# Moving a weight conversion from ScalarE to GpSimd and shifting it in the order of steps

## The chip, the cores and the metric

The kernel runs on one core of a Trainium2 chip. The metric is the device time of one execution in microseconds; shorter is better. The engines that matter are TensorE (PE), VectorE (DVE), ScalarE (ACT) and GpSimd (POOL); SyncE (SP) issues the transfers.

## The reference

Causal attention with 2 batches, 12 heads, 448 tokens and 64 columns a head, then two feed-forward layers on the 896 x 768 result:

```python
attn = softmax(where(causal, q @ k.T / 8, -1e9)); x = attn @ v
h = x @ w_in                 # 768 -> 2048
y = (h * cos(h)) @ w_out     # 2048 -> 768
out = ((y @ w_a) * (y @ w_b)) @ w_out2   # 768 -> 1536 -> 768
```

The weights arrive as 64-bit floats, everything else as 32-bit floats.

## The kernel before

A product is made of three matmul terms on reduced 32-bit floats (fp32r): each operand is split into a high part `hi` and a rest `lo`, and hi*hi, hi*lo and lo*hi are summed in PSUM (`product`, line 160).

The weights come in 70 chunks of up to 128 x 768 numbers, each as pairs of 32-bit words, and are converted on the chip. One chunk goes through these functions: `w_load` (DMA by SP's queue), `w_scale` (ACT rescales the high word in place), `w_shift` and `w_pack` (DVE brings the mantissa bits together in the low word), `w_sign` (DVE adds the sign), `w_hi` (ACT copies the low word, read as a float, into `w_hi`, rounded to fp32r), and `w_lo` (POOL subtracts `w_hi` from it, and then the load of chunk i + 3 is issued). So `w_sign`, `w_hi` and `w_lo` of a chunk are a chain. There are three `w_raw` buffers and four pairs `w_hi`, `w_lo`.

`w_pump` (line 135) makes the next half of this work: on one call shift and pack of a chunk, on the next one sign, hi and lo of this chunk and scale of the chunk behind it.

Attention runs first, in steps written out by hand (`CYCLE`, line 464): four steps, called banks, for each of 12 pairs of heads. Each engine takes its instructions in the order in which they are written. `scores` puts products into four PSUM banks, one for each of the steps; `row_max` (DVE) reads them, `exps` (ACT) makes the exponentials and sums, `recip` (DVE) the reciprocals, `scale_p` (POOL) multiplies, `transposes` (PE) turns the result into two PSUM banks, `keep` (DVE and ACT) copies these out, and `values` (PE) multiplies by v. The seven row tiles of a pair are in two groups, even tiles (6, 0, 4, 2: the first two banks) and odd ones (5, 3, 1: the last two). `scale_p`, `transposes` and `keep` exist for either group.

`ASIDE` (line 483) puts other work behind the `CYCLE` work of a step. Chunk 0 is converted at steps 5 to 10. `PUMPS` (line 495) names the steps of four calls of `w_pump`: shift and pack of chunk 1; sign, hi, lo of chunk 1 and scale of chunk 2; shift and pack of chunk 2; sign, hi, lo of chunk 2 and scale of chunk 3. `ROWS` puts parts of the first three w_in products between the steps from 44 on; the third of them, which reads chunk 2, begins at step 53. The last scores are issued at step 44.

Behind attention come the rest of w_in with the cosine gate, w_out, w_a with w_b, and w_out2, each with a call of `w_pump` per unit of work.

Of the kernel before, what the change touches and what calls it, by code (L numbers as in the profile page):

```python
# [12 lines left out]
ACTF = mybir.ActivationFunctionType  # L13
ALU = mybir.AluOpType
# [7 lines left out]
def f32(ap):  # L22
    return ap.bitcast(F32)
# [3 lines left out]
def tile_causal_attention_cos_gate_bilinear(  # L27
# [16 lines left out]
    nc = tc.nc  # L44
# [18 lines left out]
    def act_tiles(pool, tag, kind, b, n):  # L63
        return [
            tuple(pool.tile([P, S], F32R, tag=f"{tag}{b}_{t}{part}", name=f"{kind}{b}_{t}{part}") for part in ("hi", "lo"))
            for t in range(n)
        ]


    CHUNK = 6 * P  # L70
    queue = []
    for kind, w in (("in", w_in), ("out", w_out), ("ab", None), ("o2", w_o2)):
        if kind == "ab":
# [2 lines left out]
        for f in range(w.shape[0]):  # L76
            for j, o in enumerate(range(0, w.shape[2], CHUNK)):
                queue.append((kind, f, j, w[f][:, o : min(o + CHUNK, w.shape[2])]))
    raw, chunks = {}, {}
    pumps = itertools.count(3)  # L80

    def w_raw():
        return wp.tile([P, CHUNK, 2], I32, tag="w_raw", name="w_raw", bufs=3)

# [35 lines left out]
    def w_hi(i):  # L120
        if i < len(queue):
            kind, f, j, src = queue[i]
            n = src.shape[1]
            pair = tuple(wp.tile([P, CHUNK], F32R, tag=f"w_{p}", name=f"w_{p}", bufs=4) for p in ("hi", "lo"))
            nc.scalar.activation(pair[0][:, :n], f32(raw[i][:, :, 0]), ACTF.Copy)  # L125
            chunks[kind, f, j] = (*pair, n // P)

    def w_lo(i, engine):
# [6 lines left out]
    def w_pump():  # L135

        i, odd = divmod(next(pumps), 2)
        if odd:
            w_shift(i)
            w_pack(i)  # L140
        else:
            w_sign(i - 1)
            w_hi(i - 1)
            w_lo(i - 1, nc.gpsimd)
            w_scale(i)
# [38 lines left out]
        yield ps  # L184


    EARLY = 3
    PARTS = 6
    units = [(f, b) for b in range(B) for f in range(EARLY)]
    units += [(f, b) for f in range(EARLY, N_IN) for b in range(B)]  # L190
    stages, partial = {}, {}
# [26 lines left out]
    def square(u):  # L218
        if u in stages:
            r = stages[u][1]  # L220
            nc.scalar.activation(r, r, ACTF.Square, scale=2.0**0.5)  # L221

    def gate(u):
        if u in stages:
            ps, r = stages[u]
            nc.vector.scalar_tensor_tensor(out=r, in0=r, scalar=1.0, in1=ps, op0=ALU.subtract, op1=ALU.mult)  # L226
# [47 lines left out]
    with ExitStack() as actx:  # L274
# [6 lines left out]
        for o in (0, S):  # L281
            for e in range(2):
                half = mask[e * D : (e + 1) * D, o : o + D]
                nc.gpsimd.affine_select(
                    out=half,
# [172 lines left out]
        def at(fn, i):  # L458
# [27 lines left out]
            (8, w_pack, 0),  # L486
            (9, w_sign, 0),
            (10, w_hi, 0),
            (10, w_lo, 0, nc.gpsimd),
            (14, w_load, 1),  # L490
# [1 line left out]
            (22, w_scale, 1),  # L492
        ]
        ROWS = [44, 45, 46, 47, 48, 49, 50, 51, 51, 52, 52, 53, 53, 54, 55, 56, 57, 57]
        PUMPS = [24, 28, 32, 36]
        WARM = 4
        for k, step in enumerate(ROWS):
            ASIDE.append((step, rows_part, k // PARTS))
        for step in PUMPS:
            ASIDE.append((step, w_pump))  # L500
# [19 lines left out]
    with tc.manual_schedule():  # L520
        g = [act_tiles(g_pool, "g", "g", b, N_IN) for b in range(B)]
        for u in range(EARLY):
            gate(u - 2)
# [3 lines left out]
            square(u - 1)  # L527
            if u < EARLY - 1:
                w_pump()
        for u in range(EARLY, len(units) + 2):  # L530
            gate(u - 2)
# [81 lines left out]
```

## Time and profile before

| what | value |
|---|---|
| median of 3 runs | 590.97 us (589.45 to 591.11) |
| the profiled execution's own time | 589.5 us |
| its span in the trace | 587.7 us |
| PE busy | 575.7 us, 98% of the span |
| DVE busy | 360.3 us, 61% |
| ACT busy | 270.0 us, 46% |
| POOL busy | 217.9 us, 37% |
| granted TensorE clock | 1.000 |

An engine's busy time is the time in which one of its instructions is in flight; a matmul that waits for an operand inside a merged row can count as busy.

### The profile page before, as it was taken

How to read it: one execution, taken by the hardware profiler on the slowest of the kernel's cores; microseconds unless marked ns; L12 is line 12 of the kernel's file. 1: busy time of each engine (PE TensorE's matmuls, PEld its weight loads, DVE VectorE, ACT ScalarE, POOL GpSimd, SP SyncE). 2: the span in 40 equal slices, each digit the busy share in tenths (PEclk: the TensorE clock that was granted, in tenths of full speed). 3: DMA queues.
4: the chain of work that ended last, by engine and by line, in shares of the span. 5: the costliest groups of instructions: out<-in, count | busy, mean ns of one | idle time of the engine just before them, and what ended most of it. 6: DMA issues, size and time to landing. Idle time of an engine off the chain costs nothing.

```text
span 587.7 us, 8729 instructions
## 1 busy us (share of the span) xinstructions
PE 575.7 (98%) x3310; PEld 512.7 (87%) x3310; DVE 360.3 (61%) x599; ACT 270.0 (46%) x534; POOL 217.9 (37%) x197
## 2 busy tenths in 40 slices
PE   8898899999999999999999999999999999999997
PEld 6565578999999999999999999999999999999996
DVE  4877764777777776644564666666666666555500
ACT  5787865777777742322232333333333333322100
POOL 4656641666666653322232222222222222322200
PEclk9999999999999999999999999999999999999999
DMA  8662410333333244332432433333323333443000
GB/s 315 255 211 83 172 45 0 109 108 107 109 107 109 90 126 161 94 113 82 144 116 99 159 109 108 107 109 107 109 107 108 109 108 108 138 139 138 32 32 31
DMA packets 15449, 67.80 MB, mean 115 GB/s; under 512 B 1712, under 2 KB 3376, under 8 KB 15408
## 3 DMA queue, kind: packets, MB, share of 16 engines
q1 hardware_dynamic: 15408, 67.25, 33.8%
q8 instruction: 26, 0.43, 0.3%
q14 instruction: 15, 0.12, 0.1%
HBM read 64.49 MB, written 2.75 MB: 114 GB/s over the span
## 4 chain that ended last, share of the span: by engine, by line
PE 93%; DVE 2%; POOL 2%; ACT 1%; issue 1%; DVEq 0%; POOLq 0%
PE h L169 20%; PE y L169 20%; PE o L169 15%; PE a L169 15%; PE b L169 15%; PE xa L434 3%; PE pt L407 2%; PE s L334 2%; ACT p L378 1%; POOL w_lo L132 1%; POOL p L393 1%; DVE p L357 1%; PE warm L454 1%; DVE pp L420 0%; DVE w_raw L103 0%
## 5 line engine op out<-in xcount | busy, mean ns | idle before, releaser
L132 POOL TENSOR_TENSOR w_lo<-w_raw,w_hi 128x768 fp32r<-128x768 f32 (+1 forms) x70 | 128.9, 1842 | 279.8 <-ACT w_hi L125 209.6
L109 DVE SCALAR_TENSOR_TENSOR w_raw<-w_raw 128x768 int32<-128x768 int32 (+1 forms) x70 | 124.4, 1777 | 63.2 <-ACT w_raw L98 62.3
L125 ACT ACTIVATE w_hi<-w_raw 128x768 fp32r<-128x768 f32 (+1 forms) x70 | 62.7, 896 | 163.7 <-DVE w_raw L116 100.6
L116 DVE SCALAR_TENSOR_TENSOR w_raw<-w_raw 128x768 int32<-128x768 int32 (+1 forms) x70 | 65.9, 942 | 0.4
L98 ACT ACTIVATE w_raw<-w_raw 128x768 f32<-128x768 f32 (+1 forms) x70 | 61.5, 878 | 0.0
L393 POOL TENSOR_SCALAR p<-p,sums 128x448 f32<-128x448 f32 (+6 forms) x84 | 41.8, 517 | 24.3 <-DVE sums L386 16.1
L378 ACT ACTIVATE p<-p,mn 128x448 f32<-128x448 f32 (+6 forms) x84 | 41.8, 499 | 13.3 <-DVE mn L357 13.3
L103 DVE TENSOR_SCALAR w_raw<-w_raw 128x768 int32<-128x768 int32 (+1 forms) x70 | 42.8, 611 | 0.0
L357 DVE CUSTOM_DVE_ANT_0 p<-s,mask 128x448 f32<-128x448 f32 (+6 forms) x84 | 32.1, 417 | 15.0 <-PE pt L407 9.7
L210 DVE SCALAR_TENSOR_TENSOR r<-k,h 128x448 f32<-128x448 int32 x32 | 19.8, 618 | 26.0 <-ACT k L209 25.6
L334 PE MATMUL s<-qk_raw 64*64 64x64 f32 (+6 forms) x336 | 30.7, 411 | 2.4 <-DVE mn L357 2.3
L563 DVE COPY o<-o 128x448 f32<-128x448 f32 x12 | 7.5, 625 | 35.3 <-PE o L169 35.3
L334 PEld LDWEIGHTS s<-qk_raw 64*64 64x64 f32 x336 | 15.4, 139 | 15.6 <-DVE mn L357 6.6
L407 PE MATMUL pt<-ident,p 128*128 128x128 f32 x168 | 23.6, 280 | 4.8 <-POOL p L393 3.8
L209 ACT ACTIVATE k<-h 128x448 int32<-128x448 f32 x32 | 17.3, 540 | 18.6 <-PE h L169 17.8
L407 PEld LDWEIGHTS pt<-ident,p 128*128 128x128 f32 x168 | 18.1, 140 | 8.3 <-POOL p L393 5.1
L555 DVE TENSOR_TENSOR c<-a,bs 128x448 f32<-128x448 f32 x24 | 15.0, 625 | 15.4 <-PE a L169 15.4
L434 PEld LDWEIGHTS xa<-pp,v 128*64 128x64 f32 x336 | 16.1, 137 | 9.0 <-issue 6.9
L434 PE MATMUL xa<-pp,v 128*64 128x64 f32 (+3 forms) x336 | 23.8, 293 | 0.0
L226 DVE SCALAR_TENSOR_TENSOR r<-r,h 128x448 f32<-128x448 f32 x32 | 19.5, 611 | 1.5 <-ACT r L221 1.5
L216 ACT ACTIVATE r<-r 128x448 f32<-128x448 f32 x32 | 18.3, 573 | 0.0
L221 ACT ACTIVATE r<-r 128x448 f32<-128x448 f32 x32 | 18.3, 571 | 0.0
(376 smaller groups left out, 1560.9 us busy)
## 6 DMA issues: line engine op xcount, KB each, us to landing
w_raw<-in_w_in SPq DMA_DIRECT2D x16, 768.0 KB, 4.3
w_raw<-in_w_out SPq DMA_DIRECT2D x12, 768.0 KB, 4.2
w_raw<-in_w_b SPq DMA_DIRECT2D x12, 768.0 KB, 4.2
w_raw<-in_w_a SPq DMA_DIRECT2D x12, 768.0 KB, 4.4
w_raw<-in_w_o SPq DMA_DIRECT2D x12, 768.0 KB, 4.3
v<-in_v SPq DMA_DIRECT2D x12, 448.0 KB, 5.8
qk_raw<-in_qk SPq DMA_DIRECT2D x11, 448.0 KB, 5.9
w_raw<-in_w_out SPq DMA_DIRECT2D x6, 512.0 KB, 3.8
```

Of the source, the lines that this page charges most:

```text
L98: nc.scalar.activation(high, high, ACTF.Copy, scale=2.0**-112)
L103: nc.vector.tensor_single_scalar(low, low, 29, op=ALU.logical_shift_right)
L109: nc.vector.scalar_tensor_tensor(out=low, in0=high, scalar=3, in1=low, op0=ALU.logical_shift_left, op1=ALU.bitwise_or)
L116: nc.vector.scalar_tensor_tensor(out=low, in0=high, scalar=SIGN, in1=low, op0=ALU.bitwise_and, op1=ALU.bitwise_or)
L125: nc.scalar.activation(pair[0][:, :n], f32(raw[i][:, :, 0]), ACTF.Copy)
L132: engine.tensor_tensor(out=lo[:, :n], in0=f32(raw.pop(i)[:, :, 0]), in1=f32(hi)[:, :n], op=ALU.subtract)
L169: nc.tensor.matmul(ps, w[:, c * P : (c + 1) * P], acts[t + c][part], start=t == 0 and i == 0, stop=t + k == n and i == len(terms) - 1,)
L334: nc.tensor.matmul(T["s", i + c][q, o : o + WIDTH[j]], t[h, Q_COL[j] : Q_COL[j] + D], t[h, FIRST[j] : FIRST[j] + WIDTH[j]], start=True, st ...
L378: nc.scalar.activation(t, t, ACTF.Exp, bias=T["mn", n][:, c], scale=-1.0, accum_out=row_sum(n, j))
L393: nc.gpsimd.tensor_scalar(out=t, in0=t, scalar1=row_sum(n, j), scalar2=1.0, op0=ALU.mult, op1=ALU.mult)
L407: nc.tensor.transpose(dst, p_bufs[n % N_P][:, o : o + P], ident)
L434: nc.tensor.matmul(ps[e * D : (e + 1) * D, o * D : w * D], t[:, k, e], p[:, :, :, q].rearrange("p s l q -> p (s l) q") if k < 3 else p[:, ...
```

## The change

`w_hi` of the first three chunks runs on POOL as a `tensor_scalar` that multiplies by 1 twice; the other 67 stay on ACT. `PUMPS` becomes 26, 32, 46, 49. `EARLY` is the constant 3 that also counts the w_in products begun inside attention; its line moves up.

```diff
+    EARLY = 3
     queue = []
...
             pair = tuple(wp.tile([P, CHUNK], F32R, tag=f"w_{p}", name=f"w_{p}", bufs=4) for p in ("hi", "lo"))
-            nc.scalar.activation(pair[0][:, :n], f32(raw[i][:, :, 0]), ACTF.Copy)
+            src = f32(raw[i][:, :, 0])
+            if i < EARLY:
+                nc.gpsimd.tensor_scalar(out=pair[0][:, :n], in0=src, scalar1=1.0, scalar2=1.0, op0=ALU.mult, op1=ALU.mult)
+            else:
+                nc.scalar.activation(pair[0][:, :n], src, ACTF.Copy)
...
-    EARLY = 3
...
-        PUMPS = [24, 28, 32, 36]
+        PUMPS = [26, 32, 46, 49]
```

## Rows read from the trace of the kernel before

**Rows 1.** The page: chain that ended last; costliest groups (busy us, mean ns).

```profile
PE 93%; DVE 2%; POOL 2%; ACT 1%; issue 1%; DVEq 0%; POOLq 0%
...
L103 DVE TENSOR_SCALAR w_raw<-w_raw 128x768 int32<-128x768 int32 (+1 forms) x70 | 42.8, 611 | 0.0
```

**Rows 2.** Busy time of each engine by stretch, with its column line.

```profile
core 0: us, PE busy (x) PEld busy (x) DVE busy (x) ACT busy (x) POOL busy (x), PEclk, DMA share, GB/s
...
27.40:95.40 68.00, 64.65 (x693) 44.65 (x689) 45.71 (x181) 47.39 (x152) 34.06 (x64) 1.00 0.32 111
95.40:110.00 14.60, 14.60 (x74) 13.54 (x73) 11.10 (x16) 12.13 (x22) 5.87 (x4) 1.00 0.16 55
```

**Rows 3.** Timeline of PE: start, length, line, [idle before <- releaser].

```profile
33.11 1.98 PE L434 MATMUL xa<-pp,v 128*64 128x384 f32 x28
...
38.87 1.98 PE L434 MATMUL xa<-pp,v 128*64 128x384 f32 x28
...
46.50 1.98 PE L434 MATMUL xa<-pp,v 128*64 128x384 f32 x28
...
53.13 1.98 PE L434 MATMUL xa<-pp,v 128*64 128x384 f32 x28
55.68 0.98 PE L407 MATMUL pt<-ident,p 128*128 128x128 f32 x7 [0.57 <-POOL p L393]
...
61.41 1.98 PE L434 MATMUL xa<-pp,v 128*64 128x384 f32 x28
...
68.04 1.98 PE L434 MATMUL xa<-pp,v 128*64 128x384 f32 x28
...
74.45 1.98 PE L434 MATMUL xa<-pp,v 128*64 128x384 f32 x28
```

**Rows 4.** Timeline of DVE, step 24 (chunk 1, shift and pack).

```profile
42.79 0.81 DVE L103 TENSOR_SCALAR w_raw<-w_raw 128x768 int32<-128x768 int32 x1
43.64 1.11 DVE L109 SCALAR_TENSOR_TENSOR w_raw<-w_raw 128x768 int32<-128x768 int32 x1
```

**Rows 5.** Timeline, step 28: chunk 1, sign on DVE and lo on POOL.

```profile
50.42 0.95 DVE L116 SCALAR_TENSOR_TENSOR w_raw<-w_raw 128x768 int32<-128x768 int32 x1
...
52.40 1.86 POOL L132 TENSOR_TENSOR w_lo<-w_raw,w_hi 128x768 fp32r<-128x768 f32 x1 [3.63 <-ACT w_hi L125]
```

**Rows 6.** POOL's groups by form (busy us, mean ns of one).

```profile
L132 POOL TENSOR_TENSOR w_lo<-w_raw,w_hi 128x768 fp32r<-128x768 f32 x64 | 120.7, 1885 | 266.5 <-ACT w_hi L125 196.3 <-PE y L169 42.6 <-PE o L169 25.1
...
L393 POOL TENSOR_SCALAR p<-p,sums 128x448 f32<-128x448 f32 x12 | 7.7, 642 | 16.0 <-DVE sums L386 8.8 <-ACT p L378 7.2
...
L393 POOL TENSOR_SCALAR p<-p,sums 128x64 f32<-128x64 f32 x12 | 4.2, 346 | 0.0
```

**Rows 7.** Timeline of DVE, POOL and PE, steps 9 to 13 (chunk 0).

```profile
18.61 0.95 DVE L116 SCALAR_TENSOR_TENSOR w_raw<-w_raw 128x768 int32<-128x768 int32 x1
...
21.68 1.86 POOL L132 TENSOR_TENSOR w_lo<-w_raw,w_hi 128x768 fp32r<-128x768 f32 x1 [2.99 <-ACT w_hi L125]
...
23.70 0.53 DVE L420 COPY pp<-pt 128x384 f32<-128x384 f32 x1
...
25.41 0.98 PE L407 MATMUL pt<-ident,p 128*128 128x128 f32 x7 [1.96 <-POOL p L393]
```

**Rows 8.** Timeline of an undisturbed pair: ACT, DVE and PE.

```profile
34.33 0.51 ACT L378 ACTIVATE p<-p,mn 128x256 f32<-128x256 f32 x1 [0.42 <-DVE mn L357]
...
35.71 0.60 ACT L418 ACTIVATE pp<-pt 128x512 f32<-128x512 f32 x1 [0.39 <-PE pt L407]
...
36.15 0.23 DVE L357 CUSTOM_DVE_ANT_0 p<-s,mask 128x64 f32<-128x64 f32 x1 [1.10 <-PE pt L407]
...
36.74 1.04 PE L407 MATMUL pt<-ident,p 128*128 128x128 f32 x7
```

**Rows 9.** Timeline of ACT and PE, steps 48, 49 and 53.

```profile
83.53 0.60 ACT L418 ACTIVATE pp<-pt 128x512 f32<-128x512 f32 x1 [1.10 <-PE pt L407]
...
84.87 0.93 PE L407 MATMUL pt<-ident,p 128*128 128x128 f32 x7
...
92.75 0.36 PE L169 MATMUL h<-x_0hi,w_hi 128*128 128x448 f32 x1
```

## The prediction

> **What bounds the kernel now.** I read the page first: the chain of waits is 93% TensorE, with 2% DVE, 2% POOL and 1% ACT [rows 1]. TensorE is therefore the bound, and a change off it is worth only the TensorE idle time that it removes. The table of windows then says where that idle time is: from 95.4 us on, in the stretch shown and in those after it up to the last outputs, TensorE is busy the whole time; between 27.4 and 95.4 us it is busy 64.65 of 68.0 us [rows 2]. So whatever attention ends earlier, the program ends earlier, as long as the projections behind it stay fed.
>
> Third came the timeline of TensorE, read by the start of `values` (line 434), one per pair of heads [rows 3]. An undisturbed pair takes 38.87 - 33.11 = 5.76 us. The five pairs after it take 7.63, 6.63, 8.28, 6.63 and 6.41 us: 35.58 us, against 28.80, so 6.78 us are lost. (The idle remarks alone show less, since a matmul that waits inside a merged row counts as busy.) These five pairs are where chunks 1 and 2 are converted, at PUMPS steps 24, 28, 32, 36. Last I read DVE, ACT and POOL around those steps, to see which instruction each lost microsecond follows.
>
> Per chunk there are three losses. Shift and pack (first pump) hold DVE between `keep` and the `row_max` of tiles 4 and 2, whose PSUM bank the next scores need: 42.79 to 44.67, 1.87 us lost out of 7.63 [rows 3, 4]. Sign (second pump) takes DVE at the same place: 0.87 us lost (6.63). Then ACT's hi, and POOL's lo behind it, keep POOL from the odd `scale_p`, and the next transposes start late: 0.65 us (6.41 - 5.76; for chunk 1 this is the 55.68 row). The 8.28 is 0.65 of chunk 1 and 1.87 of chunk 2, to the hundredth. Sum: 3.39 us per chunk.
>
> **The change, part by part.**
>
> *Chunk 2's shift and pack, from step 32 to 46.* It removes 1.87 us. At step 46 no scores are left to be issued, and w_in matmuls stand between TensorE's attention pieces. What is late next: the `row_max` and Exp of tiles 3 and 1, and behind them ACT's copy of transposes (`keep`), whose bank the next transposes need. That copy sat waiting 1.10 us for TensorE at 83.53; a delay of 1.85 makes it 0.75 late, 84.28, and it ends at 84.88; the transposes start at 84.87 [rows 9]. So cost 0, with no margin; if the Exp is later than I read, it costs up to 1.87 again.
>
> *Chunk 2's sign, hi, lo, from step 36 to 49.* Removes 0.87 + 0.65. At step 49 DVE does sign behind `x_hi` and `x_lo`, about half a microsecond each after that copy, so from 85.9 to 86.85 (0.95, as at 50.42); POOL has only the last `scale_p` left ahead of it, and hi and lo end near 86.85 + 0.9 + 1.9 = 89.65 on the old clock. The first matmul that reads this chunk stands at 92.75 [rows 9], lo only later: slack above 3 us. Cost 0. Chunk 3's scale goes to step 49 with it, on an ACT that has nothing but copies left: 0. In SP's queue the load of chunk 5 no longer stands ahead of the last two v loads, and comes behind everything; it has the whole first projections to land: 0.
>
> *Chunk 1's shift and pack, from step 24 to 26.* They now stand behind the even `keep`, ahead of `row_max` of tiles 3 and 1. In an undisturbed pair DVE idles 1.10 us soon after that point, and the scores that need the bank come late enough. But Exp of tiles 3 and 1 moves from 34.33 to 36.18, ACT is done with it 1.85 later than 35.22 (0.51 and 0.39 after 34.33), at 37.07, and its copy ends at 37.67 instead of 36.31. The even transposes, which stood at 36.74, need that bank [rows 8]: 0.9 us late. DVE's and ACT's remaining lateness fits in their idle time of the next pair. So 0.9 in place of 1.87: a gain of 1.0. Ends: 0 lost (the copy frees the bank in time) to 1.87 (no better than before).
>
> One measured thing enlarges these two instructions: beside POOL's `scale_p` the shift took 0.81 us, against a mean of 0.61 over the kernel [rows 1, 4]. At steps 26 and 46 the even `scale_p`, four tiles, starts right before them, so I keep 1.85 for both. [...]
>
> *Chunk 1's sign, hi, lo, from step 28 to 32.* The same place in the cycle of four steps, so sign costs 0.87 again. Then hi runs on POOL in place of ACT. In the trace sign ended at 51.37 (50.42 + 0.95) and lo began at 52.40, 1.03 later, with ACT's hi between them [rows 5]. POOL's hi is not in the trace (one input, 768 columns, every second word). Nearest rows: `scale_p`, the same operation with two multiplies, takes 642 ns for 448 columns and 346 ns for 64, so 0.77 ns a column: 346 + 704 x 0.77 = 0.89 us. The other end is lo, two inputs and the same strided source: 1.885 us [rows 6]. I take 0.9, since operation and input count are those of `scale_p`, plus 0.05 for the step to lo. So lo starts where it did: change 0, ends +0.05 to -0.95. ACT is 0.9 us freer there, but the late transposes followed POOL, not ACT. The load of chunk 4 goes from step 28 to 32 in SP's queue and holds back the last q/k load and one v load, needed eight and more steps later: 0.
>
> [...]
>
> *Chunk 0's hi, step 10.* Here ACT was in the way: sign ends at about 19.5 on DVE, but ACT comes to hi only after its Exps, and POOL waits 2.99 us, until 21.68, to start lo; then four `scale_p` tiles, then the transposes at 25.41, TensorE having idled 1.96 [rows 7]. On POOL, hi starts at 19.5, lo at 20.45 to 20.55: 1.1 to 1.2 earlier, and everything in that chain follows. `keep` on DVE, which frees their second bank, began at 23.70 and took 0.53, ahead of the new start at 24.3, so 1.1 us gained. With hi at 1.885 it is 0.15.
>
> **Sum.** 1.1 + 1.0 + 0 + 3.39 = 5.5 us. The profiled execution took 589.5 us (span 587.7 and 1.8 around it): 584.0. That execution lies 1.5 below the median of the runs shown, 590.97, from which it would be 585.5. I predict between the two: 584.8. With the ends of the terms alone (step 26 costing 0 to 1.87, hi 0.89 to 1.885) the likeliest case runs from 582.8 to 587.5.
>
> **Rivals.** Differences under 0.3%, 1.8 us, cannot be told from no change here.
>
> 1. *The gain comes out half.* hi on POOL takes as long as lo, 1.885: chunk 0 gains 0.15, chunk 1 loses 0.95; 5.5 - 1.9 = 3.6, 586.7. For it: the strided source. Against: lo's second input explains its length.
>
> 2. *Step 26 and 46 are no better places than 24 and 32.* Shift and pack each wait for a `scale_p` tile of up to 0.64 us, and the Exp behind them goes late by over 2.5 us: 1.87 stays at step 26 (-1.0) and 1.0 to 1.9 comes back at 46; gain 2.6 to 3.5, about 587.3. For it: the copy at step 46 has no margin. Against: beside three `scale_p` tiles both together took only 1.88 [rows 4].
>
> 3. *Nothing moves.* The projections take the gain back, waiting for chunks 3 to 5. 590.3, within 0.3%. Against: POOL, ACT and DVE idle there [rows 2], and these chunks keep their distance to their matmuls.
>
> 4. *Slower.* POOL runs in order, so at steps 10 and 32 each microsecond of hi delays lo, `scale_p` and the transposes by one: the price is 2 us per us of hi. The gain of 5.5 is gone where hi takes 0.9 + 2.75 = 3.65 us, and above 4.6 us the kernel is over 0.3% slower; 5 us give 592.6. For it: a copy on POOL that rounds to fp32r from strided words has no row. Against: lo rounds to fp32r from the same words in 1.885 [rows 6].
>
> **How the numbers follow.** Forecast 0.64; rival 1 0.11; rival 2 0.13; rival 3 0.06; rival 4 0.06. The range runs from 582.6, the low end of the likeliest case, to 588.4, which takes in rivals 1 and 2 and leaves out 3 and 4. Faster by over 0.3%: 0.64 + 0.11 + 0.13 = 0.88, less 0.01 for an unlucky sum of both, 0.87; same 0.08; slower 0.05 (a part of rival 4 lies within 0.3%).
>
> **What would show it.** POOL's hi near 0.9 us, in three rows. The starts of `values`: after the chunk 0 conversion everything 1.1 earlier; one pair with 0.9 lost (step 26), one with 0.87, one with 0.65, all others at 5.76; first unbroken h matmuls at 89.9 instead of 95.4. No TensorE idle ahead of the matmuls of w_in's third block. The prediction is wrong if hi is above 1.9 us, if the pair of step 26 takes 7.6 us again, or if the h stage shows idle TensorE.

## The result, and the profile after

The changed kernel takes **584.51 us** (median of 4 runs, 583.57 to 584.54) against 590.22 us (4 runs, 589.45 to 591.11) for the kernel before, run on the same chip: 0.9898 of its time, 95% interval 0.9886 to 0.991. The forecast was 584.8 us, in a range of 582.6 to 588.4. The profiled execution took 584.54 us, 4.96 less than the profiled one of before.

From the page of the changed kernel, the busy times and the chain that ended last; the span is 582.7 us. In the changed kernel the lines of before stand two to six further down: `values` is L439, the transposes L412, shift L105, pack L111, sign L118, lo L138, `row_max` L362, `scale_p` L398; hi on GpSimd is L129.

```profile
PE 573.5 (98%) x3310; PEld 513.1 (88%) x3310; DVE 360.7 (62%) x599; ACT 267.0 (46%) x531; POOL 221.4 (38%) x200
...
PE 94%; DVE 2%; ACT 2%; POOL 1%; issue 1%; DVEq 0%; POOLq 0%
```

GpSimd's share of the chain went from 2% to 1% and ACT's from 1% to 2% [rows 1]. By line, ACT's share is that of its Exps, which now wait for DVE at step 26. The two stretches that answer to [rows 2] and have its columns, 5.2 us earlier each:

```profile
22.20:90.20 68.00, 65.66 (x728) 47.09 (x726) 50.53 (x202) 49.63 (x165) 40.78 (x75) 1.00 0.41 136
90.20:104.80 14.60, 14.60 (x74) 13.55 (x73) 11.11 (x16) 12.14 (x22) 5.88 (x4) 1.00 0.16 55
```

TensorE is again busy the whole time from the second stretch on, and that stretch begins at 90.20 instead of 95.40 (89.9 was forecast). Nothing behind attention gave the gain back.

The timeline of TensorE, answering to [rows 3], [rows 7] and [rows 9]: the start of each pair's `values`, and the transposes that waited.

```profile
19.73 1.98 PE L439 MATMUL xa<-pp,v 128*64 128x384 f32 x28
...
24.36 0.99 PE L412 MATMUL pt<-ident,p 128*128 128x128 f32 x7 [0.92 <-POOL p L398]
...
26.30 1.98 PE L439 MATMUL xa<-pp,v 128*64 128x384 f32 x28
...
43.58 1.98 PE L439 MATMUL xa<-pp,v 128*64 128x384 f32 x28
...
48.09 0.95 PE L412 MATMUL pt<-ident,p 128*128 128x128 f32 x7 [0.51 <-ACT pp L423]
...
50.06 1.98 PE L439 MATMUL xa<-pp,v 128*64 128x384 f32 x28
...
54.57 0.52 PE L412 MATMUL pt<-ident,p 128*128 128x128 f32 x3 [0.22 <-DVE pp L425]
...
57.05 1.98 PE L439 MATMUL xa<-pp,v 128*64 128x384 f32 x28
...
59.65 0.98 PE L412 MATMUL pt<-ident,p 128*128 128x128 f32 x7 [0.62 <-POOL p L398]
...
63.49 1.98 PE L439 MATMUL xa<-pp,v 128*64 128x384 f32 x28
...
69.25 1.98 PE L439 MATMUL xa<-pp,v 128*64 128x384 f32 x28
...
75.06 1.98 PE L439 MATMUL xa<-pp,v 128*64 128x384 f32 x28
...
79.66 0.93 PE L412 MATMUL pt<-ident,p 128*128 128x128 f32 x7
...
81.11 1.98 PE L439 MATMUL xa<-pp,v 128*64 128x384 f32 x28
...
87.54 0.36 PE L175 MATMUL h<-x_0hi,w_hi 128*128 128x448 f32 x1
```

From the timeline of TensorE before, the starts of `values` that [rows 3] leave out, the first two and the two behind those shown there:

```profile
19.75 1.98 PE L434 MATMUL xa<-pp,v 128*64 128x384 f32 x28
...
27.35 1.98 PE L434 MATMUL xa<-pp,v 128*64 128x384 f32 x28
...
80.27 1.98 PE L434 MATMUL xa<-pp,v 128*64 128x384 f32 x28
...
86.32 1.98 PE L434 MATMUL xa<-pp,v 128*64 128x384 f32 x28
```

Subtracting neighbours gives the pairs: chunk 0's takes 26.30 - 19.73 = 6.57 us (before 7.60), three pairs of 5.76 lead to 43.58, and then come 6.48, 6.99, 6.44 and 5.76. Where five pairs lost 6.78 us, three now lose 0.72 + 1.23 + 0.68 = 2.63. Chunk 2's shift and pack now stand in the pair from 75.06. It takes 81.11 - 75.06 = 6.05 us, the same as without them before (86.32 - 80.27), and the transposes at 79.66 show no wait.

The timeline of GpSimd: hi and lo of the three chunks.

```profile
19.63 0.91 POOL L129 TENSOR_SCALAR w_hi<-w_raw 128x768 fp32r<-128x768 f32 x1 [0.95 <-DVE w_raw L118]
20.61 1.87 POOL L138 TENSOR_TENSOR w_lo<-w_raw,w_hi 128x768 fp32r<-128x768 f32 x1
...
55.38 0.90 POOL L129 TENSOR_SCALAR w_hi<-w_raw 128x768 fp32r<-128x768 f32 x1 [2.57 <-DVE w_raw L118]
56.37 1.85 POOL L138 TENSOR_TENSOR w_lo<-w_raw,w_hi 128x768 fp32r<-128x768 f32 x1
...
81.53 0.91 POOL L129 TENSOR_SCALAR w_hi<-w_raw 128x768 fp32r<-128x768 f32 x1
82.53 1.87 POOL L138 TENSOR_TENSOR w_lo<-w_raw,w_hi 128x768 fp32r<-128x768 f32 x1
```

hi takes 0.91 us where lo, from the same words, takes 1.87 [rows 6]; in chunk 0, lo starts at 20.61 and no longer waits 2.99 us for ACT until 21.68 [rows 7]. The last lo ends at 84.40, 3.1 us ahead of the first matmul of that chunk's product, at 87.54.

### The profile page after: what moved, and what is told of

Read it like the earlier page. It is cut to its first block, busy times and chain, and to the rows that moved or that the text cites. A ratio compares the mean times of both kernels' runs of the same rounds, so it can differ in the third digit from the quotient of the medians.

```text
span 582.7 us, 8735 instructions
## 1 busy us (share of the span) xinstructions
PE 573.5 (98%) x3310; PEld 513.1 (88%) x3310; DVE 360.7 (62%) x599; ACT 267.0 (46%) x531; POOL 221.4 (38%) x200
## 4 chain that ended last, share of the span: by engine, by line
PE 94%; DVE 2%; ACT 2%; POOL 1%; issue 1%; DVEq 0%; POOLq 0%
PE h L175 20%; PE y L175 20%; PE o L175 15%; PE a L175 15%; PE b L175 15%; PE xa L439 3%; PE pt L412 3%; PE s L339 2%; ACT p L383 2%; DVE p L362 1%; PE warm L459 1%; POOL p L398 1%; DVE pp L425 0%; POOL w_lo L138 0%; DVE w_raw L118 0%
## 5 line engine op out<-in xcount | busy, mean ns | idle before, releaser
L138 POOL TENSOR_TENSOR w_lo<-w_raw,w_hi 128x768 fp32r<-128x768 f32 (+1 forms) x70 | 128.9, 1841 | 264.8 <-ACT w_hi L131 194.1
L111 DVE SCALAR_TENSOR_TENSOR w_raw<-w_raw 128x768 int32<-128x768 int32 (+1 forms) x70 | 124.1, 1772 | 63.2 <-ACT w_raw L100 62.3
L131 ACT ACTIVATE w_hi<-w_raw 128x768 fp32r<-128x768 f32 (+1 forms) x67 | 59.9, 895 | 163.2 <-DVE w_raw L118 100.0
L118 DVE SCALAR_TENSOR_TENSOR w_raw<-w_raw 128x768 int32<-128x768 int32 (+1 forms) x70 | 65.9, 941 | 0.4
L398 POOL TENSOR_SCALAR p<-p,sums 128x448 f32<-128x448 f32 (+6 forms) x84 | 42.5, 527 | 27.3 <-DVE sums L391 16.9
L105 DVE TENSOR_SCALAR w_raw<-w_raw 128x768 int32<-128x768 int32 (+1 forms) x70 | 42.7, 610 | 0.0
L362 DVE CUSTOM_DVE_ANT_0 p<-s,mask 128x448 f32<-128x448 f32 (+6 forms) x84 | 31.9, 416 | 13.1 <-PE pt L412 8.0
L339 PE MATMUL s<-qk_raw 64*64 64x64 f32 (+6 forms) x336 | 28.5, 410 | 0.3 <-DVE mn L362 0.2
L412 PE MATMUL pt<-ident,p 128*128 128x128 f32 x168 | 23.7, 279 | 3.9 <-POOL p L398 2.2
L412 PEld LDWEIGHTS pt<-ident,p 128*128 128x128 f32 x168 | 18.1, 140 | 7.5 <-POOL p L398 3.1
L439 PE MATMUL xa<-pp,v 128*64 128x64 f32 (+3 forms) x336 | 23.8, 293 | 0.0
L439 PEld LDWEIGHTS xa<-pp,v 128*64 128x64 f32 x336 | 16.1, 137 | 8.7 <-issue 6.8
```

Of the source, the lines that this page charges most:

```text
L105: nc.vector.tensor_single_scalar(low, low, 29, op=ALU.logical_shift_right)
L111: nc.vector.scalar_tensor_tensor(out=low, in0=high, scalar=3, in1=low, op0=ALU.logical_shift_left, op1=ALU.bitwise_or)
L118: nc.vector.scalar_tensor_tensor(out=low, in0=high, scalar=SIGN, in1=low, op0=ALU.bitwise_and, op1=ALU.bitwise_or)
L131: nc.scalar.activation(pair[0][:, :n], src, ACTF.Copy)
L138: engine.tensor_tensor(out=lo[:, :n], in0=f32(raw.pop(i)[:, :, 0]), in1=f32(hi)[:, :n], op=ALU.subtract)
L339: nc.tensor.matmul(T["s", i + c][q, o : o + WIDTH[j]], t[h, Q_COL[j] : Q_COL[j] + D], t[h, FIRST[j] : FIRST[j] + WIDTH[j]], start=True, st ...
```

## The experiments

All are edits of the changed kernel. Pairs are read as above, by the starts of `values`; a ratio is to runs of the kernel before taken along with the experiment. Medians of different experiments come from different occasions; where a difference is small, the pairs decide.

**1. The new steps alone, hi on ACT again.**

```diff
-            if i < EARLY:
+            if i < 0:
```

> The new steps 26, 32, 46, 49 with every hi on ScalarE as before. Theory (the moves of chunk 2 and of chunk 1's shift and pack carry 4.15 us of the gain, chunk 0's hi 1.03): 4.1 to 4.2 us faster than before, the pair of chunk 0 at 7.6 us again, the pairs behind it as in the changed kernel (6.5, 7.0, 6.4, then 5.8). Rival (hi on GpSimd is what frees the pair of step 32, too): at most 3.2 us faster, with the pair of step 32 longer by 0.9.

Measured: 585.63 us, ratio 0.9929 (0.9916 to 0.9943). From step 26 on the pairs are 6.49, 6.98, 6.40, 5.76, 5.81: those of the changed kernel within 0.04. So the steps carry the 4.2 us, and hi on GpSimd at step 32 is neutral. But chunk 0's pair took 9.21 us, not 7.6. Its table of windows (the number ahead of the DMA share is the granted clock):

```profile
24.00:26.00 2.00, 1.65 (x7) 1.34 (x7) 1.63 (x6) 0.70 (x4) 2.00 (x5) 0.60 0.96 353
26.00:28.00 2.00, 2.00 (x19) 1.30 (x20) 0.73 (x5) 1.80 (x7) 1.47 (x4) 0.54 0.27 104
```

and the transposes in it, from the timeline of TensorE:

```profile
24.35 1.74 PE L412 MATMUL pt<-ident,p 128*128 128x128 f32 x7 [1.95 <-POOL p L398]
```

After 1.95 us of idle time the seven transposes took 1.74 us instead of 0.98, at a granted clock of 0.60 and then 0.54. The profiled execution of before had the same idle time (1.96 us [rows 7]) and kept its clock (1.00 from 24 to 28 us), so such a gap doesn't always cost it.

**2. hi on GpSimd alone, at the old steps.**

```diff
-        PUMPS = [26, 32, 46, 49]
+        PUMPS = [24, 28, 32, 36]
```

> hi of the first three chunks on GpSimd, steps 24, 28, 32, 36 as before. Theory: 1.0 us faster than before, all of it in the pair of chunk 0 (7.6 to 6.6 us), the five pairs of chunks 1 and 2 at 35.6 us as before, within 0.2. Rival (ScalarE's freed 0.9 us counts at each chunk): 2 to 3 us faster.

Measured: 588.51 us (8 runs), ratio 0.9974 (0.9964 to 0.9984). Chunk 0's pair is 6.55, and the five behind it come to 35.64 us against 35.58 before. So hi is worth chunk 0's 1.0 us, and nothing for chunks 1 and 2. The medians differ by 1.46 us; against the runs of before with a mean clock of 0.999 and more (589.4 us, last section) it is 0.9.

**3. Only chunk 2 late.**

```diff
-        PUMPS = [26, 32, 46, 49]
+        PUMPS = [24, 28, 46, 49]
```

> hi on GpSimd, chunk 1 at steps 24 and 28 as before, chunk 2 at 46 and 49. Theory: 1.0 of chunk 0 and 3.4 of chunk 2, so 4.4 us faster than before; three disturbed pairs, with 1.87, 0.87 and 0.65 us lost. Two explanations of the 1.23 us that the pair of step 32 lost in the changed kernel stand against each other: if it comes from hi on GpSimd, the second disturbed pair loses 1.2 here as well; if it is an echo of shift and pack at step 26 or a place of step 32, it loses 0.87.

Measured: 585.27 us, ratio 0.992 (0.9906 to 0.9933); pairs 7.63, 6.63, 6.46, 5.76, 5.76, 5.81. Chunk 1's losses are back at their old size, within 0.05 us, and chunk 2's are gone without a trace: 3.39 us. Sign costs 0.87 here with hi on GpSimd behind it, so the 1.23 of the changed kernel isn't hi's doing.

**4. hi of chunks 0 and 1 done twice on GpSimd.**

```diff
-                nc.gpsimd.tensor_scalar(out=pair[0][:, :n], in0=src, scalar1=1.0, scalar2=1.0, op0=ALU.mult, op1=ALU.mult)
+                for _ in range(2 if i < 2 else 1):
+                    nc.gpsimd.tensor_scalar(out=pair[0][:, :n], in0=src, scalar1=1.0, scalar2=1.0, op0=ALU.mult, op1=ALU.mult)
```

> The changed kernel with hi of chunks 0 and 1 done twice in a row on GpSimd (the same result written again). Theory (GpSimd's order makes the price 1 us per us of hi at each of the two chunks): 0.9 to 1.0 us lost at each, 1.8 to 2.0 us slower than the changed kernel, about 3.2 us faster than before. Rival (the lateness is partly absorbed): under 1.0 us slower than the changed kernel.

Measured: 587.57 us, ratio 0.9955 (0.9942 to 0.9968). hi went from 0.91 to 1.91 us; both transposes behind it wait 0.99 us longer:

```profile
25.00 0.98 PE L413 MATMUL pt<-ident,p 128*128 128x128 f32 x7 [1.91 <-POOL p L399]
...
62.92 0.98 PE L413 MATMUL pt<-ident,p 128*128 128x128 f32 x7 [1.61 <-POOL p L399]
```

So the price is one for one in each of the two places, as rival 4 had it. The third microsecond of the median is the clock again. In its table of windows:

```profile
26.00:28.00 2.00, 2.00 (x18) 1.30 (x20) 0.93 (x5) 1.92 (x7) 2.00 (x5) 0.50 0.55 209
```

Behind 1.91 us of idle time TensorE's granted clock was 0.50 from 26 us on, and 0.66 in the next 2 us. The two pairs from there on lost 1.62 us more than the later hi explains. Three of the five runs have the lower mean clock, 0.997; the other two took 586.5 us, 2.0 more than the changed kernel. Behind the 1.61 us of idle time at 62.92 no row shows such a stretch: the next `values` took 1.98 us, where those at 27.82 took 2.72.

**5. Chunk 2's shift and pack at 42, under the last scores.**

```diff
-        PUMPS = [26, 32, 46, 49]
+        PUMPS = [26, 32, 42, 49]
```

> The changed kernel with chunk 2's shift and pack at step 42 in place of 46: the same place in the cycle of four, but one pair earlier, with scores still to come and no w_in matmuls between. Theory (the place behind the last scores is free, the same place ahead of them is not): 0.7 to 0.9 us slower than the changed kernel, lost in the pair of step 42 as at step 26 (0.72). Rival (the place in the cycle alone decides, step 46 is as good as 42): under 0.2 us.

Measured: 584.67 us, ratio 0.9895 (0.988 to 0.991). The pair of step 42 takes 6.09 us: 0.28 more than in the changed kernel, between the two expectations. The timeline of TensorE, the scores and the transposes behind shift and pack:

```profile
71.81 1.16 PE L339 MATMUL s<-qk_raw 64*64 64x384 f32 x12
...
73.62 0.93 PE L412 MATMUL pt<-ident,p 128*128 128x128 f32 x7
```

The w_in matmuls that start at step 44 stand ahead of these transposes, which show no wait; ACT's copy ended at 73.34. The 0.28 stands in the scores, whose row takes 1.16 us here and 0.88 in an undisturbed pair. Steps behind the scores are the better place, but by a third of what I took.

**6. Chunk 1's sign two steps earlier.**

```diff
-            w_sign(i - 1)
+            if i != 2:
+                w_sign(i - 1)
...
+            (30, w_sign, 1),
```

> The changed kernel with chunk 1's sign taken out of step 32 and put at step 30 (behind the even keep, where DVE idles 1.1 us soon after); hi and lo stay at step 32. Theory (sign loses at step 32 because row_max of tiles 4 and 2 stands behind it, and hi and lo lose because they wait for sign while scale_p waits behind them): the pairs of step 32 and after fall from 6.99 and 6.44 to 6.0 or less each, 1.3 to 1.9 us faster than the changed kernel. Rival (POOL has no room for 2.8 us of hi and lo wherever sign is): the 0.65 stays, at most 0.9 us faster.

Measured: 583.06 us, ratio 0.9873 (0.9856 to 0.9889), pairs 6.49, 6.72, 5.76. That is 1.45 us under the changed kernel by the medians, within the expectation, and 0.94 by the pairs. The pair behind lo loses nothing now, but the pair that holds sign, hi and lo still loses 0.96, more than expected. On the timeline of GpSimd and then DVE, sign stands beside `scale_p`, each holds up the other, and behind them an addition of `recip` stands beside hi:

```profile
50.12 2.54 POOL L399 TENSOR_SCALAR p<-p,sums 128x448 f32<-128x448 f32 x4 [1.54 <-DVE sums L392]
...
50.42 1.15 DVE L118 SCALAR_TENSOR_TENSOR w_raw<-w_raw 128x768 int32<-128x768 int32 x1
...
52.96 0.57 DVE L391 TENSOR_SCALAR sums<-sums 128x3 f32<-128x3 f32 x1 [0.15 <-ACT p L384]
```

Sign took 1.15 us instead of 0.95 [rows 5], the four tiles of `scale_p` 2.54 instead of 1.84, and the addition 0.57 instead of 0.17 (experiments 9 to 11). How the 0.96 is made up of these and of what step 26 leaves behind (experiment 8) isn't shown.

**7. As 6, and shift and pack in steps of their own.**

```diff
-            w_shift(i)
+            if i != 1:
+                w_shift(i)
...
+            (22, w_shift, 1),
+            (30, w_sign, 1),
```

> As the one with sign at step 30, and chunk 1's shift at step 22, its pack alone at 26, so that DVE gets under 1 us of weights at one time. Theory (one instruction of under 1 us fits in the slack of a pair, two do not): the 0.72 of step 26 goes too, all pairs from step 22 to 42 at 5.8 to 5.9 us, 2.0 to 2.6 us faster than the changed kernel. Rival (each such instruction costs its own part, about 0.36): no faster than the one with sign at step 30.

Measured: 582.44 us, ratio 0.9862 (0.9847 to 0.9877). The pair with the shift takes 5.76, that with the pack 6.04, that with sign 6.72: 1.39 us less lost than in the changed kernel. The median is 2.07 lower, inside the 2.0 to 2.6 expected, but the theory failed for two of the three instructions: the shift fits in the slack of its pair, pack alone costs 0.28, and sign's pair loses the same 0.96 as in experiment 6.

**8. Chunk 1's sign, hi and lo one cycle later.**

```diff
-        PUMPS = [26, 32, 46, 49]
+        PUMPS = [26, 36, 46, 49]
```

> The changed kernel with chunk 1's sign, hi and lo at step 36 in place of 32, so that a pair lies between them and shift and pack at step 26. It tells where the 0.36 us comes from that the pair of step 32 lost over the 0.87 of sign. If it is an echo of step 26: the pair behind that of step 26 loses 0.36 by itself (6.1 us), the one of step 36 only 0.87. If sign and the echo need each other: 5.76 for the pair between, then 6.63 and 6.4, and the kernel is 0.36 us faster than the changed one. If it is not of step 26: 5.76, then 7.0.

Measured: 584.33 us, ratio 0.989 (0.9875 to 0.9905). The timeline of TensorE:

```profile
49.93 1.98 PE L439 MATMUL xa<-pp,v 128*64 128x384 f32 x28
...
56.05 1.98 PE L439 MATMUL xa<-pp,v 128*64 128x384 f32 x28
...
62.67 1.98 PE L439 MATMUL xa<-pp,v 128*64 128x384 f32 x28
```

The pair behind that of step 26 holds no conversion now and still takes 56.05 - 49.93 = 6.12 us: 0.36 are an echo of step 26. Sign's pair takes 62.67 - 56.05 = 6.62, a loss of 0.86, and the pair behind it 6.48. This is the first of the three explanations in the expectation.

**9. Shift, pack and sign at the third step of the cycle.**

```diff
+            (23, w_shift, 1),
+            (31, w_sign, 1),
...
-        PUMPS = [26, 32, 46, 49]
+        PUMPS = [27, 32, 46, 49]
```

(The two exceptions for chunk 1 in the pump stand as in experiment 7.)

> As the spread version, but chunk 1's shift, pack and sign one step later each (23, 27, 31): behind row_max of tiles 3 and 1 and ahead of that of tile 6, right where DVE idles 1.1 us, and so no longer ahead of the Exps whose lateness held the even transposes. Theory (what is lost at steps 26 and 30 is lost through these Exps and ACT's copy): no pair from step 22 to 42 loses over 0.2 us, 2.0 to 2.6 us faster than the changed kernel, about 1.2 faster than the spread version. Rival (each instruction waits for a scale_p tile of POOL and then overruns the 1.1 us): 0.3 to 0.5 lost at pack and at sign, at most 0.5 faster than the spread version.

Measured: 582.02 us, ratio 0.9859 (0.9846 to 0.9873); pairs 5.76, 5.76, 6.41, 5.76. Shift, pack and sign, each at a step of its own, are free. The 0.65 at step 32 stayed, so the median is only 0.4 us under that of experiment 7, not 1.2, and the timeline (GpSimd, DVE, DVE, TensorE) shows why:

```profile
52.00 0.94 POOL L129 TENSOR_SCALAR w_hi<-w_raw 128x768 fp32r<-128x768 f32 x1
...
52.15 0.82 DVE L392 TENSOR_SCALAR sums<-sums 128x3 f32<-128x3 f32 x1
...
53.10 0.53 DVE L427 COPY pp<-pt 128x384 f32<-128x384 f32 x1
...
53.77 0.52 PE L414 MATMUL pt<-ident,p 128*128 128x128 f32 x3 [0.52 <-DVE pp L427]
```

An addition to three columns of sums, 0.17 us elsewhere, took 0.82, until hi was done; the copy of transposes stood behind it, and the next transposes waited 0.52 for that.

**10. The same for chunk 0: scale at 10, shift 11, pack 15, sign 19, hi and lo 20.**

```diff
-            (5, w_scale, 0),
-            (6, w_shift, 0),
-            (8, w_pack, 0),
-            (9, w_sign, 0),
-            (10, w_hi, 0),
-            (10, w_lo, 0, nc.gpsimd),
+            (10, w_scale, 0),
+            (11, w_shift, 0),
+            (15, w_pack, 0),
+            (19, w_sign, 0),
+            (20, w_hi, 0),
+            (20, w_lo, 0, nc.gpsimd),
```

> The one before, and chunk 0 spread in the same way: scale at step 10, shift 11, pack 15, sign 19, hi and lo 20. Theory (the 0.8 us that chunk 0's pair still loses in the changed kernel, 6.57 against 5.76, is hi and lo waiting for sign ahead of scale_p): that pair at 5.8 to 5.9, 0.7 to 1.2 us faster than the one before, and no TensorE idle of 0.9 us at 24 us. Rival (that pair is bound by the first loads and Exps, not by chunk 0): under 0.3 us.

Measured: 579.71 us, ratio 0.9822 (0.9809 to 0.9836), 2.3 us less than experiment 9, more than either expectation. Up to the last scores (step 44) every pair is 5.81 or less but for the two with hi, 6.39 and 6.41, where the addition took 0.80 and 0.82. Chunk 0's pair fell to 5.76, as expected, but its hi now costs 0.63 two pairs later, so the pairs together save only 0.16 us. The rest comes ahead of the first `values`. The timeline of TensorE, the first transposes and the first `values`:

```profile
11.46 0.98 PE L414 MATMUL pt<-ident,p 128*128 128x128 f32 x7 [0.65 <-POOL p L400]
...
17.71 1.98 PE L441 MATMUL xa<-pp,v 128*64 128x384 f32 x28
```

That stretch takes 6.25 us; in experiment 9, as in the changed kernel, it takes 8.01 (11.36 to 19.37). So chunk 0's conversion at steps 5 to 9 held up the steps ahead of the first `values` by 1.76 us, a loss that neither the prediction nor the expectation had looked for.

**11. As 10, without the addition.** It adds 1e-9 to sums that are at least 1 (the largest exponential of a row is 1), which changes no 32-bit number.

```diff
-            nc.vector.tensor_scalar_add(t, t, 1e-9)
```

> The version with both chunks spread, without the tensor_scalar of recip that adds 1e-9 to the row sums (this addition is left out; the reciprocal stays). In the two pairs that still lose 0.63 and 0.65 us this instruction of 3 columns took 0.80 and 0.82 us, as long as POOL's hi beside it ran. [...] Rival (what delays keep is the step's other work, the reciprocal waits in its place): both pairs stay at 6.3 to 6.4, at most 0.4 us faster.

Measured: **577.31 us** (577.07 to 577.89), ratio 0.9779 (0.9765 to 0.9792), the fastest of all. On its page TensorE is busy 99% of the span.

The pairs with hi, from 28.06 and from 45.08, now take 5.58 and 5.57 us, where the rival had 6.3 to 6.4. The pair behind chunk 0's hi and lo, from 33.64, takes 5.86; why isn't shown. The kernel is 2.4 us faster than experiment 10, more than the 0.63 and 0.65 that the pairs with hi lost there, since nearly every other pair shrank too: from the first `values` to the last, its trace is 2.1 us shorter. The timeline of TensorE:

```profile
28.06 1.98 PE L440 MATMUL xa<-pp,v 128*64 128x384 f32 x28
...
33.64 1.98 PE L440 MATMUL xa<-pp,v 128*64 128x384 f32 x28
...
39.50 1.98 PE L440 MATMUL xa<-pp,v 128*64 128x384 f32 x28
...
45.08 1.98 PE L440 MATMUL xa<-pp,v 128*64 128x384 f32 x28
```

33.64 - 28.06 and 45.08 - 39.50 are 5.58 us, where every undisturbed pair so far took 5.76. (The first pair, 5.93, and those that hold w_in matmuls didn't shrink.)

## Why the prediction was right

| step | predicted gain, us | measured | shown by |
|---|---|---|---|
| chunk 0, hi on GpSimd | 1.1 | 1.03 | experiments 1, 2 |
| chunk 1, shift and pack at 26 | 1.0 | 0.79 | experiments 1, 8 |
| chunk 1, sign, hi, lo at 32 | 0 | -0.03 | experiments 1, 3, 8 |
| chunk 2 at 46 and 49 | 3.39 | 3.39 | experiment 3 |
| sum | 5.5 | 5.2 | |

*hi on GpSimd.* The estimate of 0.9 us, from the columns of `scale_p` [rows 6], was met: the three take 902, 906 and 910 ns. This was the number on which rivals 1 and 4 hung. At chunk 0 the chain moved as a whole, and the idle time ahead of the transposes went from 1.96 [rows 7] to 0.92 us.

*Chunk 2.* The step said to have no margin had 0.3 us of it. Timeline of ACT, the copy of transposes behind shift and pack at step 46:

```profile
78.80 0.57 ACT L423 ACTIVATE pp<-pt 128x512 f32<-128x512 f32 x1
```

The copy ended at 79.37, the transposes came at 79.66. Rival 2 had DVE waiting for `scale_p` tiles here. The timeline of DVE and GpSimd shows that it was mostly the other way round:

```profile
75.48 2.85 POOL L398 TENSOR_SCALAR p<-p,sums 128x448 f32<-128x448 f32 x4 [1.10 <-DVE sums L391]
...
75.78 0.75 DVE L105 TENSOR_SCALAR w_raw<-w_raw 128x768 int32<-128x768 int32 x1
76.57 0.96 DVE L111 SCALAR_TENSOR_TENSOR w_raw<-w_raw 128x768 int32<-128x768 int32 x1
```

The four tiles of `scale_p`, 1.84 us in an undisturbed pair, took 2.85 beside shift and pack (2.86 at step 26), so GpSimd bore most of the wait, where it had room; the shift took 0.75, against a mean of 0.61 [rows 1]. The next instruction of DVE began 1.66 us after the shift did (1.68 at step 26). That is 0.2 less than the 1.85 that I kept, and most of the margin.

*Step 26.* The path was the predicted one: Exp late, ACT's copy late, the transposes at 48.09 waiting 0.51 for it. They stand 48.09 - 43.58 = 4.51 us behind the `values` of their pair, against 36.74 - 33.11 = 3.63 in an undisturbed one [rows 3, 8], so they were 0.88 late, as forecast (0.9). Of this 0.16 was made good behind them, and the pair lost 0.72.

Two sentences of this step failed. One is that "the scores that need the bank come late enough": the row of scores from 46.40 took 1.18 us, not 0.88. At step 26 the later copy covers this; in experiment 5, where the copy is in time, it is the whole loss of 0.28. The other is that the remaining lateness "fits in their idle time of the next pair": 0.36 came back one pair later. There the transposes at 54.57 waited for `keep` on DVE, which stood behind a `row_max`:

```profile
53.46 0.23 DVE L362 CUSTOM_DVE_ANT_0 p<-s,mask 128x64 f32<-128x64 f32 x1 [1.01 <-PE pt L412]
```

It began 3.40 us behind the `values` of its pair (50.06), against 36.15 - 33.11 = 3.04 in an undisturbed one [rows 3, 8]. That such an echo exists, and its size, is shown by experiment 8; why that `row_max` was late isn't, and stays open.

*Step 32.* The pair lost 1.23, of which 0.36 are the echo; that leaves 0.87 for sign, and lo cost 0.68, against 0.87 and 0.65. The part left to chance, that hi on GpSimd takes as long as the hand-over through ACT did, came out (6.98 and 6.40 with ACT, 6.99 and 6.44 with GpSimd).

*Rival 3.* The second stretch of the windows has TensorE busy 14.60 of 14.60 us, as before: the projections took nothing back. Only 0.2 us were lost behind the last copy of outputs, which starts 5.2 us earlier (578.67, before 583.88); its transfer took 2.0 us from issue to landing in both traces, and where the 0.2 went isn't shown. With the 5.2 that makes the 5.0 of the spans (587.7 to 582.7).

*The median.* It fell by 5.7 us, the profiled executions by 5.0. The forecast of 584.8 met the median closely by luck: from the profiled execution of before my sum gives 584.0, from the median that I knew 585.5, and I stood between the two without a reason from the trace for that place. What lies between these bases is TensorE's granted clock (0.999 and more in runs of 589.4 to 589.5 us, 0.997 in runs of 589.9 to 591.1: last section), a cause that the prediction didn't have.

*The sums.* Two figures don't come out of the terms as stated. The likeliest case should run from 583.1 (589.5 less the gains 1.1, 1.87 and 3.39) to 588.4 (590.97 less 0.15 and 3.39, plus the loss of 0.95), not from 582.8 to 587.5. And rival 4's 5 us of hi gives 593.0 from the 590.3 of the other rivals, not 592.6. Neither changes what the runs say of a rival. And the 44.67 at which shift and pack are said to let DVE go is the start of the `row_max` behind them, not among [rows 4]; pack's own row ends at 44.75.

## What to carry to other kernels

Price a moved conversion by the one wait that it delays last, in a cycle that has several places: here the same DVE instructions cost 1.87 us at one step, 0.72 + 0.36 at the second and, one at a time, nothing at the third of four, and behind the last scores nothing either. Look one period further than the pair that you move into, since a delay that seems to fit in idle time can come back there. Look at the start of the program too: chunk 0's conversion there cost more than its pair showed. And look for tiny instructions on the path of a busy stretch: two additions of three and four columns cost each undisturbed pair 0.19 us.

## What the runs showed of the hardware

**Behind a gap of 1.9 us the clock fell in two profiled executions and stayed in a third.** The timed runs of the kernel before fall into two groups: a mean granted clock of 0.997 with 589.9 to 591.1 us, or 0.999 and more with 589.4 to 589.5 us. Of the 37 such runs taken along with the experiments 27 were of the lower kind; the medians of the two groups lie 1.2 us apart. Experiments 1 and 4 show the place: TensorE idles 1.9 us ahead of chunk 0's transposes, and then two windows of 2 us each show a granted clock of 0.50 to 0.66, at a price of 1.6 us in the pairs. Why the groups of before lie less far apart isn't shown. The length of the gap alone doesn't decide: the profiled execution of before kept its clock (1.00) behind 1.96 us. Of the kernels with 0.9 us of idle time there or less (the changed one, and experiments 2, 3 and 5 to 11) no run fell to 0.997 (two runs of experiment 9 had 0.998, and were its shortest). Moving chunk 0's hi therefore also took away a loss that appears in some runs only.

**A small DVE addition took until the GpSimd instruction beside it ended; the reciprocal behind it didn't.** The addition to the sums takes 0.17 us alone (the median of its 24 in the kernel before). In the changed kernel it stands beside hi and beside lo:

```profile
19.93 0.62 DVE L390 TENSOR_SCALAR sums<-sums 128x4 f32<-128x4 f32 x1
...
56.91 1.34 DVE L390 TENSOR_SCALAR sums<-sums 128x4 f32<-128x4 f32 x1
```

It ends when hi (20.54) or lo (58.22) does. Experiment 11 shows that this wait was what the pairs with hi lost in experiment 10. The reciprocal of the same sums shows no such wait: in the changed kernel it took 0.18 us at 20.59, beside the lo that runs from 20.61 to 22.48, and 0.18 at 58.28, beside `scale_p`. And GpSimd's rows get longer as well: four tiles of `scale_p` took 2.85 and 2.86 us beside shift and pack instead of 1.84.

**An undisturbed pair wasn't TensorE's own time.** I took 5.76 us as the floor. Without the addition it is 5.57 to 5.58, so 0.19 us of waiting for others were inside each pair, although the timeline showed TensorE nearly without idle remarks: waits inside a merged row count as busy. The time came out of two rows: the even transposes went from 1.04 [rows 8] to 0.98 us, and the scores behind them from 1.22 to 1.09.
